# Sums and similarities ahead of a pair's first score, and the first turn's weight sums on GpSimd

## The chip, the cores and the metric

The kernel runs on one core of a Trainium2 chip. The metric is the device time of one execution in microseconds (us); lower is better. The engines of the core are named as in the profile: PE (TensorE, matrix products; PEld is its weight load), DVE (VectorE), ACT (ScalarE), POOL (GpSimd) and SP (SyncE, which here only issues transfers). Each engine works through its own queue in order, and an instruction that waits for a semaphore holds up all that stand behind it on its engine.

## The reference

Two blocks stand one behind the other. The first is attention with a cluster mask: for each of 4 batches and 8 heads, 768 queries and keys of 64 columns are each given to one of 16 clusters (the centroid of the highest cosine), and a query sees only the keys of its own cluster.

```python
q_assign = argmax(einsum(q_n, c_n)); k_assign = argmax(einsum(k_n, c_n))
mask = q_assign[..., :, None] == k_assign[..., None, :]
scores = where(mask, q @ k.T / sqrt(64), -1e9)
attn = exp(scores - max); attn = attn / sum(attn)
x = attn @ v                      # laid out as 3072 rows of 512
```

The second is a mixture of experts without dropped tokens: each of the 3072 rows goes to the one expert of 8 with the highest gate logit.

```python
logits = x @ w_gate; e = argmax(logits); gate_w = softmax(logits)[e]
y = gate_w * (relu(x @ w1[e]) @ w2[e])       # w1: 512 x 1024, w2: 1024 x 512
```

## The kernel before

**Pairs.** Attention runs in 16 pairs of heads, numbered n = 0 to 15; a batch has four pairs, 4b to 4b+3. A pair has two halves of the queries (h = 0, 1), each with six blocks of keys (j = 0 to 5). For each of these twelve blocks `score` puts the products of q and k (f32) and of the one-hot cluster rows (bf16) in a PSUM tile `sps` (three buffers), and ACT takes the exponential into a tile A (L445). `add_up` (DVE, L451) adds the six tiles of a half to `acc`, which later gives the denominators: five adds a half, none at j = 0. After the twelve come the attends (L457): A times v for both halves, in two PSUM banks, copied out to `oT` by ACT (L464).

**Work between.** The place of all other work is written out by hand: `at_pair(n, u, f, ...)` hangs a function on slot u of pair n. Slots 0 to 11 follow the twelve scores (slot h*6 + j, after that block's add), slot 12 stands between the attends of the two halves, slot 13 behind them. Functions of one slot run in the order in which they were hung there. The whole stage stands under a manual schedule: each engine's queue has the order of this text. The functions that matter here:

- `prepare(n, step)` makes pair n ready. Step 0 (`turn`): two DVE transpositions of q and k (L277). Step 1 (`similar`, L291): PE products of q and k with the centroids. Step 2 (`assign0`, `assign1`) and step 3 (`assign2`): DVE finds the one-hot rows of the best cluster, `ohT`. Steps 4 and 5 (`place`, L340 and L337): ACT copies them to mk and mq, eight copies.
- `sum_up(n)` (L480): PE sums the rows of `acc` of both halves and multiplies `oT` with the gate weights, in one PSUM bank. `weights_of(n)` (L489 to L504): DVE turns that bank and forms the reciprocals and the gate logits.
- `rows(n)` (DVE, L510) and `store(n)` (SP, L517): the pair's output goes to DRAM as rows.
- For each batch b: `gate`, `gate_exp` (ACT), `gate_sum`, `choose`, `count` (two small PE products), `number`. They choose the expert of every row and its place in the expert's list. `number` ends with six scatters by POOL (L607).
- Near the end: `rank_first` (DVE, L642) chooses the two experts of the two early turns from batches 0 to 2. `first_turns` loads their numbers into SP's registers, fetches the row lists (`places`) and asks for the first expert's weights w1 and w2. `indices`, `gather` (POOL, L738), `weigh` (DVE, L755), `take` (SP), `turn_rows` (L780) and `x_sums` bring the first turn's 288 rows into place, and `w1_sums` forms four sums of blocks of w1, 128 x 1024 each (L789).

The PSUM pool `mps` has two banks, which sum_up, similar and the attends of the two halves use in turn. PE's queue holds sum_up of pair n-1 and then similar of pair n+1 behind the third score of pair n (slot 2).

**Turns.** Then ten turns of the experts follow: two early ones of 288 rows, and eight ranked by size. A turn has two layers; most products are done as seven instead of eight block products, which need sums of blocks of w1, w2 and the rows (L968, L1069, L1088 on PE). The first turn's first layer carries in its hooks what is left of pair 15 and of batch 3: sum_up, weights_of, gate, choose, count, number, rows, store, and the gather for the second turn.

Of the kernel before, what the change touches and what calls it, by code (L numbers as in the profile page):

```python
# [33 lines left out]
def kernel(  # L34
# [11 lines left out]
    nc = tc.nc  # L46
# [121 lines left out]
    with tc.manual_schedule(), ExitStack() as actx:  # L168
# [12 lines left out]
        def load(n):  # L181
            b, hp = divmod(n, HP)
            for d, src, name in ((QIN, q, "q_in"), (KIN, k, "k_in")):
                t = d[n] = ld.tile([P, NI, Q4], F32, name=name)
                for r in range(4):
                    s = src[b, 2 * hp + r // 2, :, Q4 * (r % 2) : Q4 * (r % 2 + 1)]
                    nc.sync.dma_start(
                        out=t[Q4 * r : Q4 * (r + 1)].rearrange("t (j a) d -> t j a d", a=4),
                        in_=s.rearrange("(a t j) d -> t j a d", a=4, j=NQ),
                    )  # L190
            if n:
                load_v(n)

        def load_v(n):
            b, hp = divmod(n, HP)
            VIN[n] = ldv.tile([P, 2, NQ, D], F32, name="v_in")
            for a in range(2):
                nc.sync.dma_start(
                    out=VIN[n][:, a], in_=v[b, 2 * hp + a].rearrange("(p j) d -> p j d", j=NQ)
                )  # L200
# [73 lines left out]
        def turn(n, w):  # L274
            src, dst, name = ((QIN, QT, "qT"), (KIN, KT, "kT"))[w]
            dst[n] = qkt.tile([P, S], F32, name=name)
            nc.vector.transpose(dst[n], src.pop(n).rearrange("p i d -> p (i d)"))  # L277
# [9 lines left out]
        def similar(n):  # L287
            ps = ps_m.tile([P, 512], F32, name="mps")
            for g in range(4):
                t = (QT, KT)[g // 2][n]  # L290
                nc.tensor.matmul(  # L291
                    ps[Q4 * g : Q4 * (g + 1), 0:HS],
                    lhsT=cT[:, n % HP].rearrange("p a c -> p (a c)"),
                    rhs=t[:, HS * (g % 2) : HS * (g % 2 + 1)],
                    start=True, stop=True,
                )
            SIM[n] = ps

        def assign0(n, part=1):

            sim = asg.tile([P, HI, 2 * C], F32, name="sim")[:, 0 : HI // part]
            nc.vector.transpose(sim.rearrange("p i c -> p (i c)"), SIM.pop(n)[:, 0 : HS // part])
            SIM[n] = sim.rearrange("p i (a c) -> p (i a) c", c=C)

        def assign1(n, part=1):
            G = 2 * HI // part
            sim = SIM[n]
            mx = asg.tile([P, 2 * HI], F32, name="mx")[:, 0:G]
            nc.vector.tensor_reduce(mx, sim, axis=AX, op=ALU.max)
            ge = asg.tile([P, 2 * HI, C], BF16, name="ge")[:, 0:G]  # L310
            nc.vector.tensor_tensor(ge, sim, mx.unsqueeze(2).to_broadcast([P, G, C]), op=ALU.is_ge)
            SIM[n] = ge

        def assign2(n, part=1):
            G = 2 * HI // part
            ge = SIM.pop(n)
            rank = asg.tile([P, 2 * HI, C], BF16, name="rank")[:, 0:G]
            nc.vector.tensor_tensor(rank, ge, first_cb[:, None, :].to_broadcast([P, G, C]), op=ALU.mult)
            top = asg.tile([P, 2 * HI], BF16, name="top")[:, 0:G]
            nc.vector.tensor_reduce(top, rank, axis=AX, op=ALU.max)  # L320
            oh = asg.tile([P, HI, 2 * C], BF16, name="oh")[:, 0 : HI // part]
            nc.vector.tensor_tensor(
                oh.rearrange("p i (a c) -> p (i a) c", c=C), rank, top.unsqueeze(2).to_broadcast([P, G, C]),
                op=ALU.is_equal,
            )
            OH[n] = asg.tile([P, HS], BF16, name="ohT")[:, 0 : HS // part]
            nc.vector.transpose(OH[n], oh.rearrange("p i c -> p (i c)"))  # L327

        def place(n, w):
            t, m = OH[n], (MQ, MK)[w][n % 2]  # L330
            for h in range(2):
                for a in range(2):
                    g = 2 * w + h
                    dst = m[D * a : D * a + Q4, HS * h : HS * (h + 1)]
                    src = t[Q4 * g : Q4 * (g + 1), :]
                    if w == 0:
                        nc.scalar.copy(dst, src)  # L337
                    else:
                        big, less = (t[Q4 * g : Q4 * (g + 1), a : a + 1] for t in (ksc2, kscn2))
                        nc.scalar.activation(dst, src, AF.Identity, bias=less, scale=big)  # L340
            if w == 0:
                OH.pop(n)
# [95 lines left out]
        def score(n, h, j):  # L438

            if n + h or j > 2:  # L440
                score_half(n, h, j, True)
            score_half(n, h, j, False)
            ps = SP.pop((n, h, j))
            A[n, h, j] = ap.tile([P, 2, HS], F32, name="A")
            nc.scalar.activation(A[n, h, j], ps[:, :, 0:HS], AF.Exp, scale=D**-0.5)  # L445

        def add_up(n, h, j):
            if j == 1:
                ACC[n, h] = accp.tile([P, 2, HS], F32, name="acc")
            first = A[n, h, 0] if j == 1 else ACC[n, h]  # L450
            nc.vector.tensor_tensor(ACC[n, h], first, A[n, h, j], op=ALU.add)  # L451
# [70 lines left out]
        def prepare(n, step):  # L522
            if not 0 <= n < NPAIR:
                return
            if step == 0:
                turn(n, 0)
                turn(n, 1)
            elif step == 1:
                similar(n)
            elif step == 2:  # L530
                assign0(n)
                assign1(n)
            elif step == 3:
                assign2(n)
            elif step == 4:
                place(n, 1)
            else:
                place(n, 0)
# [285 lines left out]
        def at_pair(n, u, f, *a):  # L824
            AT.setdefault((n, u), []).append(lambda: f(*a))

        for n in range(NPAIR):
            if n:
                at_pair(n, 2, sum_up, n - 1)
                at_pair(n, 4, rows, n - 1)  # L830
                at_pair(n, 4, store, n - 1)
            for u, step in ((2 if n else 6, 1), (5 if n else 7, 2), (7 if n else 8, 3), (11, 4), (11, 5)):
                at_pair(n, u, prepare, n + 1, step)
        for b in range(B - 1):
            n = HP * (b + 1)
            last = b == B - 2
            at_pair(n, 5 if last else 10, gate, b)
            at_pair(n, 8 if last else 11, gate_exp, b)
            at_pair(n + (not last), 9 if last else 3, gate_sum, b)
            at_pair(n + (not last), 10 if last else 9, choose, b)  # L840
            at_pair(n + 2 - last, 2, count, b)
            at_pair(n + 2 - last, 3 if last else 6, number, b)
        for n in range(1, NPAIR):
            at_pair(n, 2, weights_of, n - 1)
        n = HP * (B - 1)
        slots = range(len(EARLY))
        at_pair(n + 1, 4, rank_first)

        def first_turns():
            for s in slots:  # L850
# [3 lines left out]
            GR[0]["w1"] = fetch1(GR[0]["e"], wa)  # L854
            GR[0]["w2"] = fetch2(GR[0]["e"], wa)

        at_pair(n + 1, 6, first_turns)
        for s in slots:
            at_pair(n + 1, 13, indices, s)
        at_pair(n + 2, 6, gather, 0)  # L860
        at_pair(n + 2, 13, weigh, 0)
        at_pair(n + 3, 1, take, 0)
        at_pair(n + 3, 4, turn_rows, 0)
        at_pair(n + 3, 6, x_sums, 0)
        at_pair(n + 3, 9, w1_sums, 0, (2, 1), nc.vector)
        at_pair(n + 3, 13, w1_sums, 0, (0, 3), nc.vector)

        def between(n, u):
            for f in AT.pop((n, u), ()):
                f()  # L870
# [4 lines left out]
        for n in range(NPAIR):  # L875
            if n + 2 < NPAIR:
                load(n + 2)
            for h in range(2):
                for j in range(NQ):
                    score(n, h, j)  # L880
                    if j:
                        add_up(n, h, j)
                    between(n, h * NQ + j)
            for h in range(2):
                for j in range(NQ):
                    attend(n, h, j)
                if h == 0:
                    between(n, 12)
                    prepare(n + 2, 0)
            between(n, 13)  # L890
        assert not AT

# [1 line left out]
    with tc.manual_schedule(), ExitStack() as ectx:  # L894
# [262 lines left out]
        n = NPAIR  # L1157
        last = NS - 1
# [356 lines left out]
```

## Time and profile before

| | |
|---|---|
| median of 3 runs | 660.47 us (659.32 to 660.57) |
| the profiled execution, its own time | 659.27 us |
| its span, first to last instruction | 657.5 us |
| TensorE's granted clock, mean | 0.998 |
| busy: PE / PEld / DVE / ACT / POOL | 98 / 64 / 75 / 52 / 20% |
| PE busy | 644.2 us |
| chain that ended last: PE / issue / DVE | 80 / 10 / 5% |
| attention ends, the turns begin (L902) | 329.47 us |

Times of the profile are counted from the first instruction. The busy share of an engine counts the time in which one of its instructions runs. A matmul's end is modelled, and the records of consecutive matmuls overlap, so the step from one start to the next says more than a duration. The same holds for DVE, where the next instruction is recorded as starting some 0.1 us before the end of the one before. In a timeline a bracket behind a line gives the time that the engine stood idle before it and what ended that wait.

### The profile page before, as it was taken

To read this page: it belongs to the slowest core of one execution; us is meant where nothing else is said; L and a number is where in the kernel's file an instruction comes from. 1 tells how busy PE (TensorE), PEld (TensorE's weight loads), DVE (VectorE), ACT (ScalarE), POOL (GpSimd) and SP (SyncE) were. 2 spreads that over 40 slices of the span, in tenths; PEclk is the share of its full clock that TensorE was granted. 3 is DMA by queue.
4 is the path that set the end of the run, shared out by engine and by line. 5 is a ranking of instruction groups with operands and counts; after the bars stand their busy time and mean duration, and the time that the engine had idled before them with its cause. 6 is when DMAs were issued, how large, how long until landed. Compare 5 with 4: busy or idle time off the path is not lost.

```text
span 657.5 us, 11491 instructions
## 1 busy us (share of the span) xinstructions
PE 644.2 (98%) x4252; PEld 423.3 (64%) x4252; DVE 490.0 (75%) x845; ACT 338.8 (52%) x584; POOL 130.8 (20%) x166
## 2 busy tenths in 40 slices
PE   8999999999999999999999999999999999999996
PEld 4444544455444454544484979989797987869773
DVE  6988888998889988989887997888869365572300
ACT  4677878768878777867532333333231331323210
POOL 4500000022000300041103522324240422140010
PEclk9999999999999999999999999999999999999999
DMA  7663455443355433347475587776684835614010
GB/s 150 150 120 68 76 94 97 72 80 68 73 97 98 74 76 72 72 132 227 117 273 156 187 314 264 252 275 211 249 307 170 273 138 165 233 74 173 7 49 19
DMA packets 189760, 95.38 MB, mean 145 GB/s; under 512 B 152895, under 2 KB 171839, under 8 KB 188416
## 3 DMA queue, kind: packets, MB, share of 16 engines
q1 hardware_dynamic: 184624, 81.56, 45.2%
q0 software_dynamic: 4928, 12.97, 6.1%
q8 instruction: 35, 0.57, 0.4%
q14 instruction: 29, 0.24, 0.1%
q10 hardware_dynamic: 144, 0.03, 0.0%
HBM read 74.10 MB, written 20.70 MB: 144 GB/s over the span
## 4 chain that ended last, share of the span: by engine, by line
PE 80%; issue 10%; DVE 5%; POOL 2%; ACT 1%; DMA 1%; POOLq 0%; DVEq 0%; ACTq 0%
PE sps L433 20%; PE mps L457 16%; PE bank L968 10%; PE sbank L968 8%; PE bank L1069 7%; PE bank L1088 7%; PE sbank L1069 6%; PE mps L480 2%; PE mps L291 1%; PE bank L937 1%; DMA xg<-x_rows,gi 1%; DVE xT L780 1%; POOL tokens_of L607 1%; DVE acc L451 1%; DVE a L789 1%
## 5 line engine op out<-in xcount | busy, mean ns | idle before, releaser
L445 ACT ACTIVATE A<-sps 128x768 f32<-128x768 f32 x192 | 152.1, 814 | 30.0 <-PE sps L433 29.4
L433 PE MATMUL sps<-qT,kT 64*128 64x384 f32 x768 | 158.9, 492 | 0.0
L451 DVE TENSOR_TENSOR acc<-acc,A 128x768 f32<-128x768 f32 x128 | 121.4, 948 | 11.4 <-ACT A L445 2.9
L457 PE MATMUL mps<-A,v_in 128*64 128x384 f32 x768 | 127.4, 488 | 0.0
L433 PEld LDWEIGHTS sps<-qT,kT 64*128 64x128 f32 x768 | 66.8, 187 | 52.2 <-issue 48.4
L457 PEld LDWEIGHTS mps<-A,v_in 128*64 128x64 f32 x768 | 53.7, 137 | 70.6 <-issue 62.9
L1043 POOL DMA_INDIRECT out_dram<-z,si x30 | 47.7, 1590 | 196.0 <-DVE z L926 167.2
L607 POOL DMA_INDIRECT tokens_of<-tg,pos_i x24 | 27.5, 1147 | 270.5 <-DVE pos_i L605 264.4
L433 PE MATMUL sps<-mq,mk 64*128 64x384 bf16 x384 | 64.9, 323 | 3.1 <-ACT mq L337 1.3
L1088 PE MATMUL bank<-w,h 128*128 128x512 f32 (+2 forms) x224 | 64.4, 596 | 0.0
L340 ACT ACTIVATE mk<-ohT,kscn,ksc 32x384 bf16<-32x384 bf16 x60 | 42.0, 700 | 40.5 <-DVE ohT L327 39.7
L968 PE MATMUL bank<-xT,w 128*128 128x144 f32 (+4 forms) x288 | 47.7, 309 | 0.0
L738 POOL DMA_INDIRECT xg<-x_rows,gi x30 | 38.4, 1280 | 47.0 <-DVE si L729 16.4
L968 PE MATMUL sbank<-xc,a 128*128 128x144 f32 (+4 forms) x288 | 47.7, 309 | 0.0
L1088 PEld LDWEIGHTS bank<-w,h 128*128 128x128 f32 (+2 forms) x224 | 24.6, 151 | 32.5 <-issue 32.3
L968 PEld LDWEIGHTS bank<-xT,w 128*128 128x128 f32 x288 | 43.8, 190 | 2.6 <-issue 2.2
L451 DVE TENSOR_TENSOR acc<-A 128x768 f32<-128x768 f32 x32 | 30.4, 952 | 19.2 <-ACT A L445 19.1
L968 PEld LDWEIGHTS sbank<-xc,a 128*128 128x128 f32 x288 | 43.4, 190 | 0.0
L926 DVE TENSOR_TENSOR h<-sbank,p 128x288 f32<-128x288 f32 (+4 forms) x18 | 9.2, 514 | 45.7 <-PE sbank L968 45.5
L433 PEld LDWEIGHTS <-mk 64*128 64x128 bf16 x384 | 19.9, 94 | 29.0 <-DVE mk L383 2.6
L986 ACT ACTIVATE h<-h 128x288 f32<-128x288 f32 (+4 forms) x36 | 17.6, 488 | 38.1 <-DVE h L926 38.1
L755 DVE TENSOR_TENSOR xw<-xg,sf 128x256 f32<-128x256 f32 (+2 forms) x60 | 32.8, 606 | 0.9 <-DMA xg<-x_rows,gi 0.6
(216 smaller groups left out, 900.5 us busy)
## 6 DMA issues: line engine op xcount, KB each, us to landing
w<-in_moe_w_dram SPq DMA_DIRECT2D x20, 2048.0 KB, 10.7
v_in<-in_v_dram SPq DMA_DIRECT2D x32, 192.0 KB, 2.5
x_rows<-x SPq DMA_DIRECT2D x64, 96.0 KB, 2.4
turn_rows<-xw SPq DMA_DIRECT2D x23, 256.0 KB, 2.0
q_in<-in_q_dram SPq DMA_DIRECT2D x60, 96.0 KB, 3.2
k_in<-in_k_dram SPq DMA_DIRECT2D x60, 96.0 KB, 3.2
xs<-turn_rows SPq DMA_DIRECT2D x16, 144.0 KB, 2.8
xs<-turn_rows SPq DMA_DIRECT2D x8, 208.0 KB, 4.2
```

The lines of the kernel that those rows point to most:

```text
L340: nc.scalar.activation(dst, src, AF.Identity, bias=less, scale=big)
L433: nc.tensor.matmul(SP[n, h, j][:, a, 0:HS], lhsT=kt[rows, j * P : (j + 1) * P], rhs=qt[rows, h * HS : (h + 1) * HS], start=first, stop=not ...
L445: nc.scalar.activation(A[n, h, j], ps[:, :, 0:HS], AF.Exp, scale=D**-0.5)
L451: nc.vector.tensor_tensor(ACC[n, h], first, A[n, h, j], op=ALU.add)
L457: nc.tensor.matmul(O[n, h][D * a : D * (a + 1), 0:HS], lhsT=VIN[n][:, a, j, :], rhs=A[n, h, j][:, a, :], start=(j == 0), stop=(j == NQ - 1),)
L607: ins = nc.gpsimd.indirect_dma_start(out=t_d[:, :], out_offset=bass.IndirectOffsetOnAxis(ap=pos_i[:, i : i + 1], axis=0), in_=tg[:, b, i, ...
L738: nc.gpsimd.indirect_dma_start(out=xg[0:m], out_offset=None, in_=x_d[0:rows_in, :], in_offset=bass.IndirectOffsetOnAxis(ap=g["gi"][0:m, j ...
L755: nc.vector.tensor_tensor(xw[0:m, :, :, d2 * a : d2 * (a + 1)], xg[0:m].rearrange("p (r a d b) -> p a r b d", r=HP, a=2, b=DB)[:, a], g["s ...
L968: nc.tensor.matmul(ps[:, f * T2 : (f + 1) * T2], lhsT=w[:, k, (2 * j + f) * P : (2 * j + f + 1) * P], rhs=x[:, k, :], start=first and f + ...
L1043: ins = nc.gpsimd.indirect_dma_start(out=out[:, :], out_offset=bass.IndirectOffsetOnAxis(ap=GR[s]["si"][0:rows, j : j + 1], axis=0), in_=z ...
L1069: nc.tensor.matmul(ps[:, 0:H], lhsT=x[:, k, :], rhs=y[:, k, :], start=first and k == 0, stop=k == 3, skip_group_check=not first,)
L1088: nc.tensor.matmul(ps[i * m : (i + 1) * m, :], lhsT=h[:, f, j * P : j * P + m], rhs=w[:, f, :], start=(k == 0), stop=(k == FB // n - 1),)
```

## The change

In pairs 2 to 15, similar of pair n+1 and sum_up of pair n-1 move from slot 2 to a new slot -1, which stands ahead of the first score; similar is now the first of the two. weights_of follows there. In pairs 0 and 1 they keep their slots (with the order of the two changed in pair 1). The two steps of the assignment move from slots 5 and 7 to 2 and 4 (pairs 0 and 1 keep theirs). The turning of q and k for pair n+2 moves from between the attends to slot 9 (pair 0 keeps slot 12). The gate work of a batch is put in other slots, for the third batch above all; rank_first moves from slot 4 to 9 and first_turns from 6 to 11 of pair 13, indices from slot 13 of pair 13 to slot 2 of pair 14, weigh and take some slots forward. The four w1_sums of the first turn leave DVE in pair 15 and stand in POOL's queue from slot 9 of pair 14 on.

```diff
         for n in range(NPAIR):
+            front = (6, 2)[n] if n < 2 else -1
+            at_pair(n, front, prepare, n + 1, 1)
             if n:
-                at_pair(n, 2, sum_up, n - 1)
+                at_pair(n, front, sum_up, n - 1)
                 at_pair(n, 4, rows, n - 1)
                 at_pair(n, 4, store, n - 1)
-            for u, step in ((2 if n else 6, 1), (5 if n else 7, 2), (7 if n else 8, 3), (11, 4), (11, 5)):
-                at_pair(n, u, prepare, n + 1, step)
+            for step, u in enumerate(((7, 8), (5, 7))[n] if n < 2 else (2, 4)):
+                at_pair(n, u, prepare, n + 1, 2 + step)
+            for step in (4, 5):
+                at_pair(n, 11, prepare, n + 1, step)
+            at_pair(n, 9 if n else 12, prepare, n + 2, 0)
         for b in range(B - 1):
             n = HP * (b + 1)
             last = b == B - 2
-            at_pair(n, 5 if last else 10, gate, b)
-            at_pair(n, 8 if last else 11, gate_exp, b)
-            at_pair(n + (not last), 9 if last else 3, gate_sum, b)
-            at_pair(n + (not last), 10 if last else 9, choose, b)
-            at_pair(n + 2 - last, 2, count, b)
+            at_pair(n, 2 if last else 10, gate, b)
+            at_pair(n, 3 if last else 11, gate_exp, b)
+            at_pair(n + (not last), 6 if last else 3, gate_sum, b)
+            at_pair(n + (not last), 7, choose, b)
+            at_pair(n + 2 - last, -1, count, b)
             at_pair(n + 2 - last, 3 if last else 6, number, b)
         for n in range(1, NPAIR):
-            at_pair(n, 2, weights_of, n - 1)
+            at_pair(n, -1 if n > 1 else 2, weights_of, n - 1)
         n = HP * (B - 1)
         slots = range(len(EARLY))
-        at_pair(n + 1, 4, rank_first)
+        at_pair(n + 1, 9, rank_first)
...
-        at_pair(n + 1, 6, first_turns)
+        at_pair(n + 1, 11, first_turns)
         for s in slots:
-            at_pair(n + 1, 13, indices, s)
+            at_pair(n + 2, 2, indices, s)
         at_pair(n + 2, 6, gather, 0)
-        at_pair(n + 2, 13, weigh, 0)
-        at_pair(n + 3, 1, take, 0)
+        at_pair(n + 2, 11, weigh, 0)
+        at_pair(n + 2, 13, take, 0)
         at_pair(n + 3, 4, turn_rows, 0)
         at_pair(n + 3, 6, x_sums, 0)
-        at_pair(n + 3, 9, w1_sums, 0, (2, 1), nc.vector)
-        at_pair(n + 3, 13, w1_sums, 0, (0, 3), nc.vector)
+        at_pair(n + 2, 9, w1_sums, 0, (2, 1, 0, 3), nc.gpsimd)
...
             if n + 2 < NPAIR:
                 load(n + 2)
+            between(n, -1)
             for h in range(2):
...
                 if h == 0:
                     between(n, 12)
-                    prepare(n + 2, 0)
             between(n, 13)
```

## The prediction

> **What bounds the kernel now.** I read the page first (engine shares, then the chain that ended last): TensorE (PE) is busy 98% of the span and carries 80% of the chain. The chain in order of time shows how one pair of heads repeats. Columns: start us, length us, what.
>
> ```profile
> 91.10 2.62 PE sps L433 x18
> 93.72 1.11 PE mps L480 x24
> 95.48 7.47 PE sps L433 x54
> 102.95 7.89 PE mps L457 x48
> 110.84 2.62 PE sps L433 x18
> ```
>
> A pair takes 110.84 - 91.10 = **19.74 us**: three scores, sum_up (L480), 0.65 us in which the chain shows nothing (the similarities, L291), nine scores, attends. All of it is PE work. The PE timeline gives the prices: a score inside a run is 0.81 (0.65 in f32, 0.16 in bf16), sum_up 1.00 (113.39 to 114.39), similar 0.65 and 0.11 more before scores follow. The cut after three scores is dear: 2.62 + 7.47 = 10.09, while twelve scores in one run, with one slow first (0.11) and one slow last (0.09), come to 9.90.
>
> VectorE (DVE) is second with 75%. Its timeline in pair 3, a pair without gate work, which began on PE at 71.29 and ended at 91.03:
>
> ```profile
> 74.12 0.96 DVE L451 TENSOR_TENSOR acc<-A 128x768 f32<-128x768 f32 x1 [2.04 <-ACT A L445]
> 75.18 0.96 DVE L451 TENSOR_TENSOR acc<-acc,A 128x768 f32<-128x768 f32 x1
> 76.06 0.38 DVE L489 STREAM_TRANSPOSE slt<-mps 128x192 f32<-128x192 f32 x1
> ...
> 85.97 4.11 DVE L451 TENSOR_TENSOR acc<-acc,A 128x768 f32<-128x768 f32 x4
> 89.99 0.97 DVE L277 STREAM_TRANSPOSE qT<-q_in 128x768 f32<-128x768 f32 x1
> 90.88 0.94 DVE L277 STREAM_TRANSPOSE kT<-k_in 128x768 f32<-128x768 f32 x1
> ```
>
> Two things are to be seen. DVE idles only 2.04 us at the head, waiting for the second exponential, and 0.20 before the third add. And its last add ends at 85.97 + 4.11 = 90.08, 0.95 before the pair ends; the two transposes after it run into the next pair. sum_up, which reads these sums, comes 2.62 us into the next pair, so the add has some 3.6 us of slack.
>
> The list of waits gives this; the first line is ScalarE (ACT) before it places the one-hots, hidden behind the attends:
>
> ```profile
> ACT mk L340 <- DVE ohT L327: 39.7, 15, 5.6
> ...
> DVE acc L451 <- ACT A L445: 22.0, 23, 2.2
> ```
>
> The longest, 5.6, is in pair 13, where number and rank_first lie on DVE: the copies of mq come late and PE stands at the head of pair 14 (4.42 us from 288.84 to the sums, where 2.63 is usual: 1.79 lost).
>
> [...] The trace has VectorE's sum of 1024 columns at 1218 ns[...]; it has no large two-input operation on GpSimd. [...] The same form on POOL, with VectorE at small work and then among the adds (17.48 to 22.65):
>
> ```profile
> 1.95 0.29 POOL masks.py:199 TENSOR_SCALAR_AFFINE_SELECT ident<-ident 128x128 f32<-128x128 f32 x1
> ...
> 19.58 1.09 POOL L147 TENSOR_SCALAR_AFFINE_SELECT lt_strict<-lt_strict 128x128 f32<-128x128 f32 x1
> ```
>
> So 0.80 of waiting for an add of 0.95. Whether adds wait for GpSimd is not seen: their step there is 1.07 against 1.05 elsewhere.
>
> **Part 1: sums and similarities ahead of the first score (pairs 2 to 15).** PE saves the cut: 10.09 - 9.90 = 0.19 a pair, so PE alone would need 19.55. But sum_up now comes before any score of the pair in PE's queue, and it needs the last add of the pair before. That closes a loop: last add, sum_up, score, exponential, first add, all the adds. I price it from S, the start of sum_up:
>
> To the first add: sum_up 1.10 with its tail; from the first score to its exponential 1.18 (115.15 to 116.33); the second exponential one step of 0.80 later, 0.81 long; 0.03 to DVE. That is 3.92. The transposition of the sums and weights_of (1.43) fit before it.
>
> From first to last add, start to start, in the new order: add 1 1.06, add 2 0.88, the first half of the assignment 1.67 (slot 2), add 3 1.07, add 4 0.87, rows 0.90, the second half 2.07 (slot 4), add 5 0.87, add 7 1.05, add 8 1.05, add 9 0.86, the two turns 1.75 (they move from after the last add to slot 9, since similar at the head wants them), add 10 1.05, add 11 0.95: 16.10. With 0.05 for the semaphore (the trace has 0.04 to 0.05 from DVE to ACT or PE) the loop is **20.07**, against 19.55 on PE and 19.74 before. VectorE, not PE, sets the pair: **+0.33** each.
>
> The copy of the second half of oT (0.48, ACT) and the bank that it frees also gate sum_up; the attends end at S + 18.89, the copy by S + 19.6, so it hides, behind similar, as long as the place copies are over. They start at S + 12.4 with the one-hots and take 4.95; they are. Their former wait thus vanishes, and so does the 1.79 at pair 14; what is late there next is the last add.
>
> **Part 2: gate, choice, numbering, ranking.** These had the idle 2.2 us and the slack of 3.6 as cover. In the loop they have none, and each counts whole, less 0.18 where it stands between two dependent adds: gate 0.60 (109.02 to 109.62), gate_sum 0.78, choose 1.37, number 1.11, rank_first 2.18; and count on PE, 0.14, follows sum_up (its bank, read by number until S + 13.8, goes to the second half's attends at S + 14.9: no wait). Batches 0 and 1: 0.42 + 0.60 + 1.19 + 1.11 + 0.14 = 3.46 each. Batch 2: pair 12 0.60 + 0.78 + 1.19 = 2.57 (its gate_exp in slot 3 makes ACT wait for gate until S + 8.1, the exponentials behind it come 2.7 late, and PE ends at about the same time as DVE; I add nothing); pair 13 0.93 + 2.18 + 0.14 = 3.25. Sum **12.74**.
>
> The chain of starts: S of pair 2 is the last add of pair 1, 50.95 + 1.56 for the turns before it, 52.56. Twelve loops 240.84 and 12.74 give 306.14 for pair 14. Pair 14 has nothing to turn, so PE sets it: its indices (0.50) fit, 19.55, 325.69. Scores and attends of pair 15 (18.89) end at 344.58; before it was 329.47 (start of L902). **+15.1.**
>
> **Part 3: weight sums to GpSimd.** Four of 1.22 leave DVE around 329 to 336. What PE lost to them in the first turn: sum_up 1.66 where 1.10 would do, 0.71 waiting for h (L926) and 0.11 for its restart, 0.21 for the count: **-1.6**. On GpSimd they come after the gathers of slot 0 and the arrival of w1. On SP the fetch stands behind two register loads that wait for rank_first, now at S + 21.4 of pair 13, and four small DMAs (2.9 from the first to the fetch, 287.49 to 290.39), so w1 is asked for some 1 us into pair 14 and lands, at 7 to 11, about when the gathers are issued. [...] behind the waiting loads SP holds only the next store, of pair 14's slot 4, so nobody waits there. Their own length therefore costs nothing. The lock can: the adds of slots 5 to 11 in pair 14 would stand behind them. [...] I take **+4**.
>
> The rest is moved at no price: load's DMAs are not reordered on SP; store stays in slot 4; take now stands ahead of the last store; turn_rows had 2.48 to wait for xs and has about that again; the later indices wait for nothing, since sf lands some 4 us into pair 14 and they come at 7.5. After the first turn all shifts along.
>
> Sum against the profiled execution (659.27): 15.1 - 1.6 + 4 = 17.5, 676.8. The median of the runs is 1.2 above it: **678.0**.
>
> **Rivals.** (a) Faster: the last add reaches sum_up in time, VectorE being quicker or the waits shorter than I chain them; then 14 x 0.19, 1.79 and 1.6 are gained: 660.5 - 6.1 = 654.4. It decides if DVE needs at most 19.55 from S to S; I have 20.07, and 1.0 more a pair on average with part 2. PE's 98% speaks for it, the 0.95 of slack at 90.08 against it: the turns alone take 1.75. (b) The loop holds, but GpSimd disturbs nothing: 674. The POOL line speaks for it. (c) The lock holds fully: 682. (d) Part 2 finds idle time after all and only the plain 0.33 counts: 12 x 0.33 + 0.3 less 1.79 and 1.6, with 4 for the lock: about 665. That the order isn't taken as written is hardly possible: the DVE timeline follows the text's order line by line.
>
> **How the numbers follow.** Main case 0.45, (b) 0.23, (c) 0.16, (d) 0.06, (a) 0.10. Range 665 to 689: (c) at 682 with 0.5 more in each of 12 loops at the top, (d) at the bottom. Faster by over 0.2% (what a measurement of this kernel can tell): (a), 0.10. Within: 0.02, between (a) and (d). Slower: 0.88.
>
> **What would show it.** Right: PE idle at each head before L480, released by DVE acc L451, small in plain pairs and 1 to 3 us after pairs 5, 9, 12 and 13; pairs of 20.1; no break among twelve scores; DVE idle about 2.5 a pair, all at the head; the wait for ohT gone. [...] Wrong: pairs of 19.55, with the last add done before similar ends.

## Result and the profile after

The changed kernel takes **687.13 us** (median; 685.39 to 688.39) against 660.07 us for the kernel before in the same session: ratio 1.0416, 95% interval 1.0399 to 1.0434. It is slower by 27 us. The forecast was 678.0 with a range of 665 to 689. The profiled execution has a span of 685.8 us (657.5 before) and a mean TensorE clock of 0.987 (0.998 before). Lines up to L800 have the numbers of before; later ones are 7 or so higher (L902 is now L909).

The page, busy times and the chain that ended last:

```profile
PE 652.3 (95%) x4252; PEld 425.9 (62%) x4252; DVE 495.6 (72%) x841; ACT 341.3 (50%) x584; POOL 142.0 (21%) x170
...
PE 62%; DVE 22%; ACT 4%; DMA 3%; issue 3%; SPq 3%; POOL 1%; DVEq 0%; POOLq 0%; ACTq 0%
```

PE has 8 us more work on record (644.2 before) and 28 us more span, and DVE's share of the chain went from 5% to 22%. So PE waits now, and what it waits for is VectorE. The chain in order of time in a plain pair (start us, length us, what):

```profile
71.52 0.78 PE mps L291 x8
72.30 1.45 PE mps L480 x24
73.75 9.89 PE sps L433 x72
83.64 7.89 PE mps L457 x48
91.53 0.78 PE mps L291 x8
```

The pair takes 91.53 - 71.52 = **20.01 us** (19.74 before; 20.07 was forecast). The twelve scores are one run of 9.89 us (9.90 was forecast): PE has its saving. But L480 takes 1.45 us where it needs 1.0, because it stands for its last operand. DVE in the same pair (start us, length us, engine, line, operation; the bracket is the idle time before it and what ended it):

```profile
76.51 0.96 DVE L451 TENSOR_TENSOR acc<-A 128x768 f32<-128x768 f32 x1 [1.27 <-ACT A L445]
...
90.56 1.98 DVE L451 TENSOR_TENSOR acc<-acc,A 128x768 f32<-128x768 f32 x2
93.81 0.38 DVE L489 STREAM_TRANSPOSE slt<-mps 128x192 f32<-128x192 f32 x1 [1.27 <-PE mps L480]
...
96.52 0.96 DVE L451 TENSOR_TENSOR acc<-A 128x768 f32<-128x768 f32 x1 [1.27 <-ACT A L445]
```

The last adds now end at 90.56 + 1.98 = 92.54, after the attends; slt follows as soon as PE has summed them; and from first add to first add it is 96.52 - 76.51 = 20.01 us with two idle times of 1.27 us, both at the head. Before, DVE's last add ended 0.95 us ahead of the pair's end and PE never asked for it there. The waits (total us, times, longest):

```profile
ACT mk L340 <- DVE ohT L327: 18.2, 14, 3.7
...
PE mps L480 <- DVE acc L451: 16.3, 7, 4.8
```

The second line was not there before; the first was 39.7 us and hid behind the attends. Two marks of the prediction did not come as written: plain pairs show no idle PE ahead of L480, only the longer L480 (idle times are 1.06 us after pairs 5, 6, 9 and 10, 0.06 after 12 and 3.08 after 13), and the wait for ohT is not gone (0.60 us in a plain pair, 2.02 before). The table sets the forecast beside the trace; pairs run from first score to first score.

| step | forecast | measured |
|---|---|---|
| plain pair | 20.07 | 20.01 |
| pairs 4, 5, 6 (20.07 and the gate work of each) | 20.49, 21.86, 21.32 | 20.85, 21.91, 21.12 |
| pairs 12, 13 | 22.64, 23.32 | 22.74, 24.32 |
| sum_up of pair 14 goes on at | 306.14 | 306.51 |
| from there to that of pair 15 | 19.55 (+4 for the lock) | 31.66 |
| from there to the end of attention | 18.89 | 21.30 |
| end of attention (L909) | 344.6 (+4) | 359.47 |
| first turn against before | -1.6 | -1.63 (360.13 to 375.57, 15.44; before 17.07) |

From layer 2 of the first turn on, the two kernels take the same: 310.2 us, and 310.3 before. Everything up to the sum_up of pair 14 is as worked out, to 0.4 us in 250. From there to the end of attention it is 14.5 us more than the 19.55 and 18.89 of the forecast, and that is two things. The first is what the prediction calls the lock: here, VectorE operations that stand while a sum runs on GpSimd. POOL in pair 14, and DVE beside it:

```profile
321.55 2.36 POOL L789 TENSOR_TENSOR a<-w 128x1024 f32<-128x1024 f32 x1
324.07 1.11 POOL L738 DMA_INDIRECT xg<-x_rows,gi  x1 [0.16 <-issue]
325.19 2.39 POOL L789 TENSOR_TENSOR a<-w,a 128x1024 f32<-128x1024 f32 x1
327.50 2.38 POOL L789 TENSOR_TENSOR a<-w 128x1024 f32<-128x1024 f32 x1
329.80 2.37 POOL L789 TENSOR_TENSOR a<-w,a 128x1024 f32<-128x1024 f32 x1
```

```profile
321.00 3.35 DVE L322 TENSOR_TENSOR oh<-rank,top 128x384 bf16<-128x384 bf16 x1
...
324.88 8.12 DVE L451 TENSOR_TENSOR acc<-acc,A 128x768 f32<-128x768 f32 x1
```

The one-hot operation of 321.00 takes 0.56 us elsewhere, the add of 324.88 takes 0.92. The first ends 0.4 us after GpSimd's first sum (323.91), the second 0.8 us after GpSimd's last (332.17), about their own lengths. So one add stood through **three** sums: 2.8 + 7.2 = 10.0 us in all. The add was not let in between one GpSimd sum and the next, though its record starts 0.31 us ahead of the first of the three. GpSimd's sums took 2.36 to 2.39 us, where VectorE took 1.22 for one in the kernel before.

The second is TensorE's clock after a wait, PE at the head of pair 14:

```profile
306.51 1.18 PE L480 MATMUL mps<-acc,ones_s 128*32 128x192 f32 x10 [3.08 <-DVE acc L451]
...
308.58 1.65 PE L433 MATMUL sps<-qT,kT 64*128 64x384 f32 x4
...
313.02 0.81 PE L433 MATMUL sps<-qT,kT 64*128 64x384 f32 x4
```

After 3.08 us of idle time the sum_up and the first scores take twice their time: 1.65 us where a first score takes 0.92 and the later ones 0.81. From the sum_up to the first add it is 6.58 us instead of 3.92. At the head of pair 15, after 4.80 and 4.18 us of idle time, the same again (2.4 us). The trace's record of the granted clock has half speed from 305.66 for 6.83 us and from 332.96 for 10.24. After waits of 1.06 us (four other heads) the first score takes 0.92.

### The profile page after: what moved, and what is told of

Read it like the earlier page. It is cut to its first block, busy times and chain, and to the rows that moved or that the text cites. A ratio compares the mean times of both kernels' runs of the same rounds, so it can differ in the third digit from the quotient of the medians.

```text
span 685.8 us, 11513 instructions
## 1 busy us (share of the span) xinstructions
PE 652.3 (95%) x4252; PEld 425.9 (62%) x4252; DVE 495.6 (72%) x841; ACT 341.3 (50%) x584; POOL 142.0 (21%) x170
## 4 chain that ended last, share of the span: by engine, by line
PE 62%; DVE 22%; ACT 4%; DMA 3%; issue 3%; SPq 3%; POOL 1%; DVEq 0%; POOLq 0%; ACTq 0%
PE bank L975 11%; PE sps L433 10%; DVE acc L451 9%; PE sbank L975 8%; PE mps L457 7%; PE bank L1095 7%; PE bank L1076 7%; PE sbank L1076 6%; PE mps L480 3%; ACT A L445 3%; DMA q_in<-in_q_dram 3%; SPq L517 2%; DVE x L510 1%; DVE xT L780 1%; DVE kT L277 1%
## 5 line engine op out<-in xcount | busy, mean ns | idle before, releaser
L451 DVE TENSOR_TENSOR acc<-acc,A 128x768 f32<-128x768 f32 x128 | 128.4, 1003 | 8.3 <-DVE acc L451 0.5
L433 PEld LDWEIGHTS sps<-qT,kT 64*128 64x128 f32 x768 | 68.8, 190 | 47.5 <-issue 43.0
L738 POOL DMA_INDIRECT xg<-x_rows,gi x30 | 40.4, 1348 | 49.5 <-DVE gi L728 18.6
L451 DVE TENSOR_TENSOR acc<-A 128x768 f32<-128x768 f32 x32 | 30.5, 954 | 23.1 <-ACT A L445 23.1
L480 PE MATMUL mps<-acc,ones_s 128*32 128x192 f32 x256 | 20.5, 352 | 16.4 <-DVE acc L451 16.3
```

The source lines that it names most:

```text
L433: nc.tensor.matmul(SP[n, h, j][:, a, 0:HS], lhsT=kt[rows, j * P : (j + 1) * P], rhs=qt[rows, h * HS : (h + 1) * HS], start=first, stop=not ...
L480: nc.tensor.matmul(ps[Q4 * qd : Q4 * (qd + 1), 0 : TC * Q4], lhsT=lhsT, rhs=rhs, start=(w == 0), stop=(w == 2),)
L738: nc.gpsimd.indirect_dma_start(out=xg[0:m], out_offset=None, in_=x_d[0:rows_in, :], in_offset=bass.IndirectOffsetOnAxis(ap=g["gi"][0:m, j ...
```

## Experiments

Each has the kernel before beside it on the same chip; the ratio is to that, with its 95% interval. e1 to e4 ran on one chip, e5 to e8 on a second, e9 and e10 on a third.

### e1: the weight sums back on VectorE

```diff
-        at_pair(n + 2, 9, w1_sums, 0, (2, 1, 0, 3), nc.gpsimd)
+        at_pair(n + 3, 9, w1_sums, 0, (2, 1), nc.vector)
+        at_pair(n + 3, 13, w1_sums, 0, (0, 3), nc.vector)
```

> The changed kernel with the four weight sums of the first turn back on VectorE in pair 15, at their old slots; all else as changed. Theory (head loop plus lock plus slow clock): the loop stays, so pair 14's sum_up again starts near 306.5 with 3 us of idle PE before it and slow products after it; but no VectorE instruction of pair 14 is stretched (the is_equal of 3.35 goes to 0.56, the add of 8.12 to 0.92), pair 15's sum_up starts some 22 us after that of pair 14 instead of 31.7, its products run at full speed, and the first turn takes 17.1 instead of 15.4. Together 687.1 - 9.5 - 2.4 + 1.6 = 677. Rival (the whole excess sits in the loop, GpSimd only fills waits that are there anyway): 686 to 689.

Measured: 679.46 us, ratio 1.0292 (1.0270 to 1.0315). No DVE operation in pair 14 is stretched, and pair 15's sum_up follows the attends at once (PE):

```profile
309.52 0.68 PE L480 MATMUL mps<-acc,ones_s 128*32 128x192 f32 x10 [3.07 <-DVE acc L451]
...
330.04 0.99 PE L480 MATMUL mps<-acc,ones_s 128*32 128x192 f32 x16
```

From one sum_up to the next it is 20.52 us instead of 31.66, and from there to the end of attention 19.03 instead of 21.30. So GpSimd's sums cost 13.4 us in these two pairs, one slow restart among them; the other is left. The total falls by less than 8 us, for three reasons.

First, sum_up of pair 14 comes 3.0 us later than in the changed kernel (309.52 against 306.51). 0.6 of it is there at the head of pair 2. 1.1 come in pair 12, where PE waits for an exponential behind gate_exp, as it does in the changed kernel (2.22 us), but here the clock is at half for 3.41 us after it (PE):

```profile
271.53 0.92 PE L433 MATMUL sps<-qT,kT 64*128 64x384 f32 x4 [2.23 <-ACT A L445]
...
272.44 1.37 PE L433 MATMUL sps<-qT,kT 64*128 64x384 f32 x4
...
273.92 1.49 PE L433 MATMUL sps<-qT,kT 64*128 64x384 f32 x4
```

The other 1.3 come in at the heads of pairs 7 and 11: the semaphore that tells of the finished sum_up moves 2.00 and 1.35 us after TensorE's recorded end (0.02 in pair 7 of the changed kernel), and DVE and ACT start with it. These late starts show again in e4 and e9, at the same two heads, and neither in the changed kernel nor in e5 to e8, which ran on another chip. So they may go with the chip and not with the edit; their cause is left open.

Second, the first turn takes 15.78 us, 0.34 more, where 1.6 more were expected. So in the new order most of the 1.63 us gained there does not hang on GpSimd. Third, from layer 2 of that turn to the end it is 312.7 us instead of 310.2, though the two kernels don't differ there.

### e2: the GpSimd sums alone, in the kernel before

```diff
-        at_pair(n + 3, 9, w1_sums, 0, (2, 1), nc.vector)
-        at_pair(n + 3, 13, w1_sums, 0, (0, 3), nc.vector)
+        at_pair(n + 2, 9, w1_sums, 0, (2, 1, 0, 3), nc.gpsimd)
```

> The kernel before, with only the four weight sums moved to GpSimd at slot 9 of pair 14. Lock theory: three or four sums of 2.4 run back to back near 301 to 311 and hold VectorE's two-input instructions for up to 10 us in pair 14; sum_up at slot 2 has about 3.6 us of slack and the place copies less, so PE stands some 6 to 8 us, restarts slowly (about 2 more), and the first turn gains 1.6: 660 + 6 to 9, near 668. Rival (GpSimd's sums hide beside VectorE): 660 - 1.6 = 658.5.

Measured: 665.78 us, ratio 1.0082 (1.0062 to 1.0102): 5.5 us slower, near the 6 to 9 of the theory, where the rival had it faster. The first turn takes 1.63 us less (16.10 instead of 17.73, L901 to the first product of layer 2), as much as in the changed kernel, and attention ends 7.9 us later (337.39). DVE in pair 14:

```profile
298.22 4.17 DVE L451 TENSOR_TENSOR acc<-acc,A 128x768 f32<-128x768 f32 x2
...
303.21 2.23 DVE L451 TENSOR_TENSOR acc<-acc,A 128x768 f32<-128x768 f32 x1
...
306.55 1.53 DVE L311 TENSOR_TENSOR ge<-sim,mx 128x384 bf16<-128x384 f32 x1
308.00 3.12 DVE L451 TENSOR_TENSOR acc<-A 128x768 f32<-128x768 f32 x1
```

Adds and sums alternate here: each of four stretches holds one sum, and GpSimd's later sums take 2.68 to 3.08 us instead of 2.38. DVE stands 2.15 + 1.31 + 0.97 + 2.17 = 6.6 us in all, more than the room of the pair. PE then waits 5.16 us at the next head (until 316.64) for the copies of mq, which follow late one-hots, and restarts slowly: the next two scores take 1.75 and 1.59 us.

### e4: TensorE kept busy while it waits

The changed kernel, with 14 and 44 bf16 products ahead of sum_up in pairs 14 and 15; they go to the PSUM tile that the first score then overwrites.

```diff
-            if first:
+            if first and (n, h, j) not in SP:
...
+        WARM = {NPAIR - 2: 14, NPAIR - 1: 44}
+
+        def warm(n):
+            t = SP[n, 0, 0] = ps_s.tile([P, 2, 512], F32, name="sps")
+            for _ in range(WARM[n]):
+                nc.tensor.matmul(
+                    t[:, 0, :], lhsT=ones_b, rhs=first_cb[:, None, :].to_broadcast([P, 512 // C, C]), start=True, stop=True,
+                )
...
+            if n in WARM:
+                at_pair(n, front, warm, n)
```

> The changed kernel with idle bf16 products (14 at the head of pair 14, 44 at that of pair 15, about 3 and 9.4 us) ahead of sum_up, in a bank that the first score overwrites, so that PE does not stand while it waits for the adds. Clock theory: after the idle stretch sum_up took 2.07 instead of 1.10 and the first two or three scores 1.6 instead of 0.81; busy, PE keeps its clock, both heads are 2.4 to 2.7 shorter: 687.1 - 5 = 682. Rival (the products after the wait are slow for another reason, such as shared memory traffic with GpSimd or late rows of mq): 687.

Measured: 684.05 us, ratio 1.0361 (1.0344 to 1.0378); the mean clock is 0.998 again. The first two scores after the wait take 0.92 and 0.81 us. The lock is as it was (an add of 8.12 us). So the slow clock at these two heads goes with TensorE's own idle time, and work that means nothing removes it. From the sum_up of pair 14 to the end of attention it is 48.07 us instead of 52.96, the 5 us that were expected. The total falls by 3.1 only, since the head of pair 14 is 2.0 us later here too (308.48): 0.9 from the head of pair 2 on, the rest by the late starts that e1 has.

### e3: sums back in slot 2, similarities ahead

e1, and sum_up, weights_of and count stand in slot 2 again.

```diff
-                at_pair(n, front, sum_up, n - 1)
+                at_pair(n, 2, sum_up, n - 1)
...
-            at_pair(n, 2 if last else 10, gate, b)
-            at_pair(n, 3 if last else 11, gate_exp, b)
+            at_pair(n, 3 if last else 10, gate, b)
+            at_pair(n, 4 if last else 11, gate_exp, b)
...
-            at_pair(n + 2 - last, -1, count, b)
+            at_pair(n + 2 - last, 2, count, b)
...
-            at_pair(n, -1 if n > 1 else 2, weights_of, n - 1)
+            at_pair(n, 2, weights_of, n - 1)
```

> The changed kernel with the weight sums on VectorE and with sum_up, weights_of and count back in slot 2 behind the third score; similar stays ahead of the first score, the turns in slot 9, the assignment in slots 2 and 4 (third batch: gate in slot 3, gate_exp in slot 4, since weights_of comes first). Loop theory: the last add has 2.5 us more, no plain pair waits for it, pairs take 19.7 to 19.9[...], only pair 13 with its ranking can still be late: 660 to 663. Rival (the turns in slot 9 or the early similarities are what costs, not where sum_up stands): 670 or more, pairs of 20 and over.

Measured: 672.74 us, ratio 1.0174 (1.0145 to 1.0202): **a miss** by 10 us; the total is the rival's, though plain pairs take 19.88 us, as the theory had it. PE no longer waits for acc by more than 0.2 us anywhere. But similar at the head has a chain of its own: it needs the PSUM bank that the copy of oT frees, and that copy stands in ACT's queue behind gate_exp, which waits 2.08 us for gate on DVE. ACT at the end of pair 4, and PE's next head:

```profile
108.37 2.08 ACT L337 COPY mq<-ohT 32x384 bf16<-32x384 bf16 x4
112.53 0.24 ACT L553 ACTIVATE ex<-ex 128x48 f32<-128x48 f32 x1 [2.08 <-DVE ex L550]
112.68 0.84 ACT L464 COPY oT<-mps 128x384 f32<-128x384 f32 x2
```

```profile
113.19 0.52 PE L291 MATMUL mps<-qT,cT 128*32 128x384 f32 x2 [1.28 <-ACT oT L464]
```

PE's waits of this kind sum to 3.5 us (as much in the changed kernel). In pair 12 PE waits 2.33 us for an exponential behind gate_exp, and the clock is at half for 3.41 us after it; that pair takes 24.17 us. These are the waits named; they and the 0.14 us more in each plain pair don't make up the whole 12.5 us. My expectation took the room behind the adds' chain to be free, and it was not. Against e1, which differs in the place of the sums and the gate work that goes with them, 6.7 of the 19 us are gone.

### e5: the sums at the head alone

```diff
-                at_pair(n, 2, sum_up, n - 1)
+                at_pair(n, -1 if n > 1 else 2, sum_up, n - 1)
...
-            at_pair(n + 2 - last, 2, count, b)
+            at_pair(n + 2 - last, -1, count, b)
...
-            at_pair(n, 2, weights_of, n - 1)
+            at_pair(n, -1 if n > 1 else 2, weights_of, n - 1)
...
+            between(n, -1)
```

> The kernel before with one part of the change alone: sum_up, weights_of and the count stand at the head of a pair, while similar, the assignment and the turns keep the places that they had. The loop theory: from the start of sum_up to the last add it is 3.92 us (start of sum_up to the first add, as in the changed kernel) and about 14.4 us of VectorE work, since the turns lie behind the last add here: about 18.3 us, under TensorE's 19.55 us, so that a plain pair stays at 19.6 to 19.9 us. Only where gate work of over 1.25 us comes in (pairs 5, 6, 9, 10, 12, 13) does the loop close, for some 5 us in all: 664 us (660 to 668). The rival, that the sums at the head are themselves what costs: plain pairs at about 20.0 us and 672 us or more.

Measured: 674.23 us, ratio 1.0222 (1.0199 to 1.0245): **a miss**; the rival's number came, plain pairs of 20.41 us. The loop is closed, though not by the last add: DVE ends it at 91.8 us, in time. It closes through ScalarE. With the assignment in slots 5 and 7, as before, the one-hots are ready late; the eight copies to mk and mq follow, then the copies of oT, and their bank is what sum_up waits for. ACT, then PE:

```profile
87.81 2.84 ACT L340 ACTIVATE mk<-ohT,kscn,ksc 32x384 bf16<-32x384 bf16 x4 [2.02 <-DVE ohT L327]
90.67 2.08 ACT L337 COPY mq<-ohT 32x384 bf16<-32x384 bf16 x4
92.76 0.86 ACT L464 COPY oT<-mps 128x384 f32<-128x384 f32 x2
```

```profile
93.30 0.86 PE L480 MATMUL mps<-acc,ones_s 128*32 128x192 f32 x16 [0.47 <-ACT oT L464]
```

PE's waits of this kind sum to 14.5 us, most of the 17.2 by which attention ends later (346.67). The longest, 3.74 us in pair 14, is followed by half speed for 3.41 us. In the first turn 1.6 us come back (15.44 us from its first product, 17.07 before), with the weight sums on VectorE. So the earlier similarities and assignment of the change have a use: they take ScalarE's chain off the sums. What remains then is the chain through the adds, 0.4 us a pair shorter.

### e6 and e7: a dose of VectorE work

In e1 (e6) and in the kernel before (e7), one more add of 128x512 at slot 8 of pairs 2 to 12, on a tile of zeros.

```diff
+        dose = consts.tile([P, 512], F32)
+        nc.gpsimd.memset(dose, 0.0)
...
+        for n in range(2, 13):
+            at_pair(n, 8, nc.vector.tensor_tensor, dose, dose, dose, ALU.add)
```

> A dose for the loop: the changed kernel with the weight sums on VectorE (679.5 us where that was run) and one more VectorE operation, an add of 128x512 f32 (about 0.63 us by the 0.92 us of the add of 128x768), at slot 8 of each of pairs 2 to 12: 11 operations. If VectorE's chain sets the length of a pair, each counts in full: 679.5 + 11 x 0.63 = 686.5 us, and the plain pair goes from 20.0 to 20.6 us. The rival, that the pairs are bound by something else (TensorE's own waits, ScalarE) and VectorE has room: 679.5 to 681 us.

> The same dose, 11 adds of 128x512 f32 at slot 8 of pairs 2 to 12, in the kernel before. The loop theory: there VectorE has some 2 us of room in a pair, so nearly nothing is to be seen: 660 to 662 us. The rival, that VectorE's work sets the pair in the kernel before too: 667 us.

Measured: e6 680.69 us, ratio 1.0314 (1.0294 to 1.0333); e7 659.14 us, ratio 0.9990 (0.9981 to 1.0000). The totals alone would speak for the rival in e6 (+1.2 instead of +7). The timeline decides otherwise. DVE in a plain pair of e6 (its L453 is the L451 of the others):

```profile
87.84 0.96 DVE L453 TENSOR_TENSOR acc<-acc,A 128x768 f32<-128x768 f32 x1
88.72 0.68 DVE L827 TENSOR_TENSOR dose<-dose 128x512 f32<-128x512 f32 x1
89.32 0.95 DVE L453 TENSOR_TENSOR acc<-acc,A 128x768 f32<-128x768 f32 x1
```

The dose is 0.68 us long on record and takes 0.60 of the queue, but 0.18 comes back: two adds to one tile in a row stand 1.06 apart, with something between them 0.88. So some 0.4 us was the dose, and the plain pair went from 20.02 to 20.42: **all of it**. In e7 the plain pair stays at 19.74, none of it. Eleven times 0.41 would be 4.5; by the end of attention 3.1 are there (352.19 and 349.07), since e6 does not have the 1.3 us of late starts of e1, and 1.7 of them are gone at the end of the experts' turns, where the two kernels don't differ. The dose is shown pair by pair; the total is no clean measure of it.

### e9: two of the four sums on GpSimd

The changed kernel with sums 2 and 1 on GpSimd, 0 and 3 on VectorE at slot 13 of pair 15.

```diff
-        at_pair(n + 2, 9, w1_sums, 0, (2, 1, 0, 3), nc.gpsimd)
+        at_pair(n + 2, 9, w1_sums, 0, (2, 1), nc.gpsimd)
+        at_pair(n + 3, 13, w1_sums, 0, (0, 3), nc.vector)
```

> Half the dose of GpSimd: the changed kernel with only the sums 2 and 1 on GpSimd (behind the gathers, as there), the sums 0 and 3 on VectorE at slot 13 of pair 15. If one VectorE operation waits through as many GpSimd sums as stand back to back, the longest add goes from 8.12 us (three sums of 2.4 us behind the fourth gather) to about 3.3 us (one sum), the stretch of 3.35 us in front of it stays, and 4.8 us come back: 682.5 us (681 to 684.5). The rival, that the long add waits for something else that falls there (the fetch of the weights landing, the slow TensorE): an add of over 6 us again and 686 us or more.

Measured: 685.09 us, ratio 1.0368 (1.0343 to 1.0394). Behind the fourth gather there is one sum now (326.58 to 328.96), and the same add waits through one (DVE):

```profile
322.39 3.35 DVE L322 TENSOR_TENSOR oh<-rank,top 128x384 bf16<-128x384 bf16 x1
...
326.27 3.52 DVE L451 TENSOR_TENSOR acc<-acc,A 128x768 f32<-128x768 f32 x1
```

3.52 us instead of 8.12, and from the sum_up of pair 14 to that of pair 15 26.05 us instead of 31.66. The add's wait goes with the number of sums that stand back to back. The total falls by only 2 us and lies just outside the 681 to 684.5 expected, because the late starts and half speed in pair 12, as in e1, put the sum_up of pair 14 2.4 us back. Both restarts are slow here too, the second after 2.36 and 2.58 us of idle time with half a microsecond of work between.

### e8 and e10: the spread alone

In the kernel before, only the preparation of the first turn is moved as in the change:

```diff
-        at_pair(n + 1, 4, rank_first)
+        at_pair(n + 1, 9, rank_first)
...
-        at_pair(n + 1, 6, first_turns)
+        at_pair(n + 1, 11, first_turns)
...
-            at_pair(n + 1, 13, indices, s)
+            at_pair(n + 2, 2, indices, s)
...
-        at_pair(n + 2, 13, weigh, 0)
-        at_pair(n + 3, 1, take, 0)
+        at_pair(n + 2, 11, weigh, 0)
+        at_pair(n + 2, 13, take, 0)
```

> The kernel before with the spread of the first turn's preparation alone: rank_first at slot 9 of pair 13 and first_turns at slot 11, indices at slot 2 of pair 14, weigh at slot 11, take behind pair 14; the weight sums stay on VectorE at slots 9 and 13 of pair 15, and the sums and the similarities where they were. Theory: the stall of 1.8 us at the head of pair 14, where VectorE is behind after rank_first, goes or shrinks, and the first turn is as before: 658.5 to 660 us. The rival, that the spread carries part of the loss (the fetches of the weights issued 5 slots later): 663 us or more.

Measured: 658.69 us, ratio **0.9986** (0.9976 to 0.9995): the one version here whose interval lies below the kernel before. PE's waits at the head of pair 14 (1.10 and 0.21 us before, for mq) are gone, and attention ends at 328.16 instead of 329.47. Half of that is lost again in the first turn (18.29 instead of 17.73 us). That this is a gain is not shown: it is under the 0.2% that is about what one can tell, and e7, which only adds work, came to 0.9990.

e10 adds one GpSimd sum to e8 (0 on POOL, 3 on VectorE at slot 13).

> The kernel before with the spread alone (658.7 us where that was run) and one sum, 0, on GpSimd, the others on VectorE at slots 9 and 13 of pair 15. One sum can hold a VectorE operation for at most its own 2.4 us, which the room of some 2 us in a pair of the kernel before covers nearly whole, and VectorE has 1.2 us less in front of the last adds and the sum_up of pair 15, where TensorE waited 0.17 us: 658.7 us, or up to 0.5 us less. The rival, that a lock costs its length wherever it falls: 660 us or more.

Measured: 660.14 us, ratio 0.9992 (0.9983 to 1.0001). The sum took 3.02 us on POOL, and attention ends at 330.30, 2.1 us later than in e8 (0.3 of it is there at the head of pair 2). Its ratio is 0.0006 above e8's, 0.4 us; the intervals overlap, so neither theory is excluded. Nothing is won by it.

## Why the prediction was right, point by point

**Direction and mechanism (part 1): right.** The loop through the last add sets the pair; the forecast 20.07 was measured as 20.01, and the dose shows it directly: 0.4 us more on DVE is 0.4 us more a pair in the new order, and nothing in the old one. Rival (a), that VectorE is in time, is out by the waits of L480 for acc.

**The gate work (part 2): right.** Seven of the eight loaded pairs came within 0.4 us; pair 13 (24.32 for 23.32) ends in the slow sum_up: 2.07 us for 1.10. Sum_up of pair 14 was 0.37 us later than forecast. Rival (d) is out.

**The weight sums (part 3): the gain right in size, the lock mis-sized.** The gain of 1.6 was 1.63. In the old order the sums alone bring it (e2). In the new order they bring 0.34 of it (e1), and e5 has it with the sums on VectorE. It may hang on how far VectorE is behind when the turn starts (its last add ends 4.2 us after attention before, 3.2 in e1, 1.5 in e5), but that was not tested.

The term that was mis-sized is "I take +4". It was the author's estimate: the kernel before has no sum of this size on GpSimd in its trace, neither its length nor what it holds up, and rival (c), the full lock, had 4 us more. Measured were 10.0 us of standing, and 31.66 - 19.55 = 12.1 us more in pair 14, of which some 2.7 are the clock: 9.4 for the lock. The 4 leaned on the one line in which the adds had won (0.80 us of waiting on POOL, none seen on VectorE), and here VectorE stood through all four. That one add is held through three sums was not foreseen, but it is not what makes the price: the four sums together last 9.5 us. e1 and e9 size it: without the sums 13.4 us come back in pairs 14 and 15, clock included; with two of them the add's wait falls from three sums to one. So rival (c), the full lock, is what came. Rival (b), no lock at all, stood at 674; e1, the nearest to it, shows 679.5, with a slow restart and the late starts on top.

**What the prediction did not have: the clock.** It priced a wait of PE at its own length. Where the wait reached 3 us, the work after it cost 2.4 to 2.7 us more, twice. By the table: end of attention 359.47 against 348.58 with the lock taken, 10.9 us: 0.4 in the loops, 8.1 in pair 14 (31.66 - 19.55 - 4, of which some 2.7 are the clock), 2.4 in pair 15 (clock). The range reached that far because it held the full lock and 0.5 us more a loop; the first was the right reason, the second was not. That 687 lies inside it is to that extent luck: the 5.1 us of the clock took the place of 6 us that did not come.

**One reading of the change was too simple.** I costed the early similarities as a help for the place copies alone. e5 and e3 show three chains that end at the head of a pair: the adds (sum_up), the mask copies with oT behind them (sum_up's bank), and oT behind gate_exp (similar's bank). Each part of the change alone shortens one and meets the next: 674.2, 672.7 and together, without GpSimd, 679.5 us.

## What to carry to other kernels

Before work is moved ahead in a queue, ask what its operands' last producer does at that moment: a consumer two microseconds after the loop's turn gives every engine that much room, and ahead of it none, though the busy shares don't change. A short dose of idle work on the suspected engine tells in one profile whether it sets the pace; read it pair by pair, not in the total. Before sums like these go to GpSimd, ask whether VectorE can stand for the whole run of them; here an add stood for three, 8.12 us for 0.92. And a wait of TensorE can cost more than its length: here 2.4 to 2.7 us more at the two heads where it waited 3.08 us and 4.80 and 4.18, and 1.1 us more after 2.23 in pair 12 of e1.

## What the runs showed of the hardware

- One VectorE add waited through three GpSimd sums in a row, 8.12 us for 0.92 (3.52 with one sum in the row), while in e2 adds and sums took turns. What decides between the two is open.
- In the changed kernel TensorE's half speed starts at 305.66, 332.96 and 684.54 us, which is 27.31 and 351.57 us apart, 8 and 103 times 3.413; the first two spells last 6.83 and 10.24 us, and those named in e1, e3 and e5 3.41. Cut in steps of 3.413 us along these starts, from 20 us on, its trace has three steps at full speed in which TensorE stood for 2.25 us or more (the third after its last product), and half speed followed each. It followed none in which TensorE stood for 1.79 us or less.
- By the waits from 20 us to the end of attention, in all twelve runs: half speed followed those of 2.23 us in e1, e6 and e9, 2.33 in e3, 3.07 to 3.09 (the changed kernel, e1, e6, e9), 3.74 in e5, 4.80 in the changed kernel and 5.16 in e2, and the 2.36 and 2.58 of e9, close together. It did not follow that of 2.22 in the changed kernel, that of 2.23 in e4, or any of 1.65 or less. In the changed kernel the 2.22 fall into two steps, 0.67 and 1.55; in e1 slow scores put the start of half speed at about 272.6, an estimate, so the wait from 269.30 to 271.53 fell into one. This is worked out from the runs after the fact; no experiment set the phase on purpose.
- Two dependent adds on one tile stand 1.06 us apart, 0.88 with another operation between: an unrelated operation of 0.6 us costs 0.41 there.
